# Attention with mixed heads and two feed-forward layers: heads paired j with j+6, queries in long rows, first values and small weights on GpSimd's queue, second keys at earlier steps

## The chip, the core and the metric

The kernel runs on one core of a Trainium2 chip. The core has five engines with an instruction queue each: TensorE (PE in the profile, PEld for its weight loads), VectorE (DVE), ScalarE (ACT), GpSimd (POOL) and SyncE (SP), which here only issues DMAs. The metric is the device time in microseconds (us); lower is better.

## The reference

Two batches, 12 heads, 448 positions, head size 64. The heads are mixed by a 12x12 matrix before the softmax and by another after it; two feed-forward layers follow.

```python
def _attn_ref(q, k, v, w_pre, w_post):
    scores = scale * np.matmul(q, k.transpose(0, 1, 3, 2))
    scores = np.einsum('bhij,hg->bgij', scores, w_pre)
    attn = np.exp(scores - np.max(scores, axis=-1, keepdims=True))
    attn = attn / (np.sum(attn, axis=-1, keepdims=True) + 1e-09)
    attn = np.einsum('bhij,hg->bgij', attn, w_post)
    return np.matmul(attn, v)
...
x = attn_out.transpose(0, 2, 1, 3).reshape(896, 768)
h = x @ w_in;    x = (h * np.clip(h + 3, 0, 6) / 6) @ w_out       # first layer, 768 -> 2048 -> 768
h = x @ w_in2;   x = (np.maximum(h, 0) + alpha * np.minimum(h, 0)) @ w_out2
```

## The kernel before

The attention works on eight tiles of query positions: in each batch three of 120 positions and one of 88. For a tile, `qk(ti, j)` multiplies queries and keys of two heads: head 2j in partitions 0 to 63 of the staging tiles `q_st` and `k_st`, head 2j+1 in partitions 64 to 127. Two results go through PSUM, and `s_out` copies them to the tile's scores `S`, one with ScalarE, one with VectorE (L551). Six values of j make a whole tile.

The scores are then regrouped. `pull(g)` is a DMA from `S` to a tile `pull` in which 10 positions x 12 heads lie in 120 partitions, so that the mixing over heads is a matrix product. Two groups make a step `p_`; there are 45 steps. A step runs `premix` (PE, L199, weights `wpre`), a maximum (DVE, L205), `exp` (ACT, L214), `norm` (L221 to L226, on GpSimd it scales `wpost` to `wr`), and one step later `post` (PE, L238), which mixes again and transposes, and `post_evac` (ACT, L253). In most steps from the seventh on there is also `av` (PE, L281) of a finished tile, which reads the values `v`, and in every step one `qk` of a later tile. Then come the two feed-forward layers: a weight block is loaded (`load_w`, L330), converted by ACT, DVE and GpSimd (L342 to L384) and multiplied in three passes (L451, `mm3`).

Each engine runs its instructions in the order in which the program is written. The DMAs of the main loop are all issued by SP, in order: at step `p_` the pulls for step `p_`+3, then what `load_at` has for this step (values of the first batch at steps 3, 5, 7 and 8; keys of the second batch at steps 10 to 13; values of the second batch later), then a query tile (`load_q_at`). A pull writes one of four buffers `d_buf` and waits until `premix` has read the old contents. A DMA of SP or ACT also takes one of eight semaphores in turn, so it waits until the eighth DMA before it has landed.

The opening, ahead of step 0: `load_k0` brings the first batch's keys in five DMAs and `load_q` the first two query tiles; the small weights `wpre` and `wraw` (60x60 blocks) come in between, on SP; GpSimd scales `wpre` and reorders `wraw` to `wpost` (L544, L545) when they have landed, and then clears the first four columns of the third query tile (L137), which TensorE needs for that tile. Two tiles are multiplied ahead of step 0, with their pulls behind the first of them.

In the host's layout `k0` holds head 2j+1 under head 2j, and `q` and `k` hold every head twice, in rows 0 to 63 and again in rows 64 to 127. From `q` a row of one head is 120 floats, that is 480 bytes, in one piece; from `k` 448 floats, 1792 bytes.

Of the kernel before, what the change touches and what calls it, by code (L numbers as in the profile page):

```python
# [12 lines left out]
ACTF = mybir.ActivationFunctionType  # L13
# [4 lines left out]
Q = 64  # L18
Z = 4
# [16 lines left out]
def kernel(  # L36
# [15 lines left out]
    nc = tc.nc  # L52
    _, D, H, S = k.shape
# [53 lines left out]
    with tc.manual_schedule():  # L107
# [4 lines left out]
        def load_k0(p, z, q=nc.sync):  # L112
            q.dma_start(out=k_st[0][:, p:z, :], in_=k0[:, p:z, :])

        def load_k(b, o, p, z):
            src = k[b - 1, D * o:D * o + D].rearrange("p (j o) s -> p j o s", o=2)
            nc.sync.dma_start(out=k_st[b][D * o:D * o + D, p:z, :], in_=src[:, p:z, o, :])
# [6 lines left out]
        load_k0(0, 1, nc.scalar)  # L124
        nc.vector.memset(three, 3.0)
        nc.vector.memset(warm, 0.0)
        nc.scalar.activation(out=warm, in_=warm, func=ACTF.Exp)
# [4 lines left out]
        def load_q(ti, *at, qs=(nc.sync, nc.sync)):  # L132
            T = tiles[ti]
            n = T["n"]
            m = H // 2 * n
            t = q_st[ti] = kq.tile([128, Z + H // 2 * GP], F32, tag="qst", bufs=2, name="qst")
            nc.gpsimd.memset(t[:, :Z], 0.0)  # L137
            z = Q + m - n + upper(n)
            if z > Z + m:
                nc.gpsimd.memset(t[:, Z + m:z], 0.0)  # L140
            at = (0, *at, H // 2)
            for x, y in zip(at, at[1:]):
                for o in range(2):
# [9 lines left out]
        def load_v(b, c):  # L153
            t = late.tile([128, HC, NJ, D], F32, tag=f"v{c}", bufs=1, name=f"v{c}")
            for a in range(2):
                nc.sync.dma_start(
                    out=t[Q * a:Q * a + JH], in_=v[b, JH * a:JH * a + JH, HC * c:HC * (c + 1)]
                )
            v_t[b, c] = t
# [3 lines left out]
        def qk(ti, j, tag="sc"):  # L163
            n = tiles[ti]["n"]
            if j == 0:
# [12 lines left out]
            return [(S_t[ti][:Z + n, 2 * j + o, :], ps[o][:Z + n, :S]) for o in range(2)]  # L178
# [344 lines left out]
        q0 = load_q(0, 1, 3, qs=(nc.sync, nc.scalar))  # L523
        next(q0)
        load_k0(1, 2)
        next(q0)
        load_k0(2, 3)
        load_k0(3, 4)
        next(q0)
        load_k0(4, H // 2)  # L530
        for c in range(2):
            a = GH * c
            nc.sync.dma_start(out=wpre[Z + GH * c:Z + GH * c + GH, :GH], in_=w_pre[a:a + GH, a:a + GH])
        q1 = load_q(1, 3)
        next(q1)
        for c in range(2):
            a = GH * c
            nc.sync.dma_start(out=wraw[Q * c:Q * c + GH], in_=w_post[a:a + GH, a:a + GH])
        next(q1)
# [3 lines left out]
        late.tile([128, 16], F32, tag="rest", bufs=1, name="rest")  # L543
        nc.gpsimd.tensor_scalar(wpre, wpre, scale, 1.0, ALU.mult, ALU.mult)  # L544
# [3 lines left out]

        def s_out(pairs):
# [3 lines left out]
        for j in range(H // 2):  # L553
            s_out(qk(0, j, ("sc", "mx")[j % 2]))
# [243 lines left out]
```

## Time and profile before

| | us |
|---|---|
| median of 3 runs (lowest, highest) | 665.51 (663.26, 666.89) |
| the profiled execution, its own time | 661.99 |
| its span, first to last instruction | 660.2 |
| PE busy in the span | 636.3 (96%) |
| DVE, ACT, POOL busy | 408.2, 353.2, 291.3 |
| attention, to the last `av` of the chain | about 202 |
| feed-forward layers | about 458 |

The profiled execution is one of its own; its time lies 3.52 us under the median of the other runs. The page's busy times are shares of the whole span, in which the attention and the feed-forward layers have different limits, so the stretches are read one by one. In a row of the timeline, the bracket at the end gives the engine's idle time just before and what ended it. "issue" there means that the engine waited for nothing that the profile shows.

### The profile page before, as it was taken

The numbers are of one execution on the slowest core, as the hardware profiler recorded it, in microseconds if no ns is written. First come the engines' busy times: TensorE is split into PE (matmuls) and PEld (weight loads), VectorE is DVE, ScalarE is ACT, GpSimd is POOL, SyncE is SP. The second block draws the span as 40 slices with busy tenths as digits, with TensorE's granted clock in tenths as the row PEclk, the third lists the DMA queues.
The fourth block names the chain that finished last, engine by engine and source line by source line (L and its number), as shares of the span: only waits on it lengthen the run. The fifth ranks groups of instructions, "written<-read, shape, count | busy, mean of one in ns | idle before, by whom it ended". The sixth has DMA issues, their size and how long they took to land.

```text
span 660.2 us, 17587 instructions
## 1 busy us (share of the span) xinstructions
PE 636.3 (96%) x7464; PEld 558.9 (85%) x7464; DVE 408.2 (62%) x640; ACT 353.2 (53%) x664; POOL 291.3 (44%) x236
## 2 busy tenths in 40 slices
PE   7996999998899999999999999999999999999997
PEld 2575776686688999999999999999999999999997
DVE  4664565756446678888543643389999998334501
ACT  4785787787774665666443443434444444443310
POOL 2121131312633445545675554445554556776430
PEclk9999999999899999999999999999999999999999
DMA  6776654654401233233343233212332223445202
GB/s 167 234 241 172 181 158 150 209 182 112 145 3 49 96 129 111 97 105 133 98 144 143 96 103 137 96 50 96 109 124 102 96 95 120 139 144 208 97 0 84
DMA packets 34923, 81.82 MB, mean 124 GB/s; under 512 B 11420, under 2 KB 24988, under 8 KB 34844
## 3 DMA queue, kind: packets, MB, share of 16 engines
q1 hardware_dynamic: 34268, 80.27, 37.3%
q8 instruction: 59, 0.97, 0.6%
q10 hardware_dynamic: 576, 0.41, 0.2%
q14 instruction: 20, 0.16, 0.1%
HBM read 58.65 MB, written 2.75 MB: 93 GB/s over the span
## 4 chain that ended last, share of the span: by engine, by line
PE 78%; ACT 6%; issue 5%; POOL 4%; DMA 3%; DVE 3%; SPq 0%; POOLq 0%; ACTq 0%; DVEq 0%
PE p L451 62%; PE pt L238 5%; PE mx L199 5%; PE av L281 4%; PE sc L174 3%; ACT e L214 3%; POOL wb L373 2%; POOL wlo L384 2%; ACT MT L253 1%; DMA kst<-in_k_dram 1%; DVE nm L205 1%; DVE xT L292 1%; DMA qst<-in_q_dram 1%; DMA pull<-S 1%; ACT S L551 1%
## 5 line engine op out<-in xcount | busy, mean ns | idle before, releaser
L384 POOL TENSOR_TENSOR wlo<-wb,whi 128x768 fp32r<-128x768 f32 x64 | 126.1, 1971 | 140.2 <-ACT whi L378 140.2
L373 POOL TENSOR_TENSOR wb<-wb,wst 128x768 int32<-128x768 int32 x64 | 125.6, 1963 | 74.5 <-DVE wb L366 64.9
L451 PE MATMUL p<-xh,whi 128*128 128x448 f32 x384 | 140.2, 365 | 0.0
L451 PE MATMUL p<-xl,whi 128*128 128x448 f32 x384 | 139.7, 364 | 0.0
L451 PE MATMUL p<-gl,whi 128*128 128x448 f32 x384 | 139.4, 363 | 0.0
L451 PE MATMUL p<-gh,whi 128*128 128x448 f32 x384 | 139.2, 362 | 0.0
L451 PE MATMUL p<-xh,wlo 128*128 128x448 f32 x384 | 138.5, 361 | 0.0
L451 PE MATMUL p<-gh,wlo 128*128 128x448 f32 x384 | 138.4, 360 | 0.1
L358 DVE TENSOR_SCALAR wb<-wb 128x768 f32<-128x768 f32 x64 | 52.0, 812 | 82.8 <-ACT wb L342 82.8
L342 ACT ACTIVATE wb<-wst 128x768 f32<-128x768 f32 x64 | 58.0, 907 | 70.2 <-DMA wst<-in_w_out_dram 52.2
L378 ACT CAST whi<-wb 128x768 fp32r<-128x768 f32 x64 | 53.3, 833 | 50.4 <-PE p L451 32.3
L238 PEld LDWEIGHTS pt<-wr,e 60*64 60x64 f32 (+1 forms) x2880 | 59.8, 135 | 22.1 <-issue 11.4
L214 ACT ACTIVATE e<-mx,nm 128x448 f32<-128x448 f32 x90 | 56.4, 634 | 39.8 <-DVE nm L205 39.7
L451 PEld LDWEIGHTS p<-xh,whi 128*128 128x128 f32 x384 | 72.3, 188 | 6.1
L451 PEld LDWEIGHTS p<-gh,whi 128*128 128x128 f32 x384 | 72.1, 188 | 5.7
L451 PEld LDWEIGHTS p<-gh,wlo 128*128 128x128 f32 x384 | 71.8, 187 | 5.5 <-POOL wlo L384 0.5
L451 PEld LDWEIGHTS p<-xh,wlo 128*128 128x128 f32 x384 | 72.0, 188 | 5.2
L226 POOL TENSOR_SCALAR wr<-wpost,sm 128x60 f32<-128x60 f32 x74 | 25.3, 356 | 115.4 <-DVE sm L222 112.8
L451 PEld LDWEIGHTS p<-xl,whi 128*128 128x128 f32 x384 | 72.4, 188 | 3.6
L451 PEld LDWEIGHTS p<-gl,whi 128*128 128x128 f32 x384 | 72.1, 188 | 3.7
L366 DVE SCALAR_TENSOR_TENSOR wb<-wst,wb 128x768 uint32<-128x768 uint32 x64 | 67.5, 1055 | 1.1
L238 PE MATMUL pt<-wr,e 60*64 60x60 f32 (+1 forms) x2880 | 60.7, 221 | 7.1 <-issue 6.1
(50 smaller groups left out, 792.4 us busy)
## 6 DMA issues: line engine op xcount, KB each, us to landing
wst<-in_w_out_dram SPq DMA_DIRECT2D x32, 768.0 KB
wst<-in_w_in_dram SPq DMA_DIRECT2D x27, 768.0 KB
pull<-S SPq DMA_DIRECT2D x88, 210.0 KB
wst<-in_w_in_dram SPq DMA_DIRECT2D x10, 384.0 KB
v<-in_v_dram SPq DMA_DIRECT2D x16, 168.0 KB
out_dram<-o SPq DMA_DIRECT2D x12, 224.0 KB
qst<-in_q_dram SPq DMA_DIRECT2D x8, 180.0 KB
kst<-in_k_dram SPq DMA_DIRECT2D x4, 336.0 KB
```

The costliest lines, as they stand in the source:

```text
L199: nc.tensor.matmul(ms[r][Q * c:Q * c + Q, :S], wpre[a:z], d[a:z, c, :], start=True, stop=True)
L214: nc.scalar.activation(out=e, in_=ms[o][:, :S], func=ACTF.Exp, bias=nms[o], accum_out=sm[:, o:o + 1])
L226: eng.tensor_scalar(wr, wpost, sm[:, o:o + 1], 1.0, ALU.mult, ALU.mult)
L238: nc.tensor.matmul(ts[c][Q * z:Q * z + m, u:u + GH], e[a:a + GH, j:j + m], wr[a:a + GH], start=True, stop=True,)
L281: nc.tensor.matmul(p[z][64 * o:64 * o + 64, a % 3, :n], v_t[T["b"], h // HC][Q * z:Q * z + JH, h % HC, t, :], MT[ti][Q * z:Q * z + JH, t, ...
L342: nc.scalar.activation(t, s[:, :, 1].bitcast(F32), ACTF.Abs)
L358: nc.vector.tensor_scalar(t, t, W_MAX, W_MIN, ALU.min, ALU.max)
L366: nc.vector.scalar_tensor_tensor(u, st_t[i][:, :, 1], 0xC0000000, u, ALU.bitwise_and, ALU.bitwise_or)
L373: nc.gpsimd.tensor_tensor(n, n, st_t.pop(i)[:, :, 0].bitcast(I32), ALU.add)
L378: nc.scalar.copy(hi, b_t[i])
L384: nc.gpsimd.tensor_tensor(lo, b_t.pop(i), w_t[i][0].bitcast(F32), ALU.subtract)
L451: nc.tensor.matmul(p, wt[a], xt[c], start=(first and z == 0), stop=(last and z == 2))
```

## The change

- Heads are paired j with j+6: partitions 0 to 63 hold head j, partitions 64 to 127 head j+6. The queries of one half are then contiguous in `q`: a row of a tile of 120 is one piece of 2880 bytes, and the separate rows of 480 bytes are gone. The host's layout stays as it is; each half is now read from its own copy alone. Keys of the second batch come in rows of three heads, 5376 bytes.
- The first batch's keys still lie two heads per 128 rows in `k0`, so each load becomes two DMAs of 64 partitions: slot 0, then slots 2 and 4, then slots 1, 3 and 5, and the first tile is multiplied in the order 0, 2, 4, 1, 3, 5. The first DMAs are split between SP and ACT; the table load of ACT comes after them.
- `wpre` and `wraw` are loaded by GpSimd's queue, after its memsets; the first batch's values follow there, after GpSimd's two operations on the small weights.
- The second batch's keys are loaded at steps 3, 5, 7 and 9.

On SP, the opening up to the first pulls, before (`kst` keys, `qst` queries, shapes are partitions x rows x floats):

```order
L147 DMA qst<-in_q_dram 64x120
L113 DMA kst<-in_k_dram 128x448
L147 DMA qst<-in_q_dram 64x2x120
L113 DMA kst<-in_k_dram 128x448 x2
L147 DMA qst<-in_q_dram 64x3x120
L113 DMA kst<-in_k_dram 128x896
L533 DMA wpre<-in_w_pre_dram 60x60 x2
L147 DMA qst<-in_q_dram 64x3x120 x2
L538 DMA wraw<-in_w_post_dram 60x60 x2
L147 DMA qst<-in_q_dram 64x3x120 x2
L189 DMA pull<-S 120x1x448 x2
```

and after:

```order
L115 DMA kst<-in_k_dram 64x448
L150 DMA qst<-in_q_dram 64x120
L115 DMA kst<-in_k_dram 64x2x448
L150 DMA qst<-in_q_dram 64x600
L115 DMA kst<-in_k_dram 64x3x448 x2
L150 DMA qst<-in_q_dram 64x720 x2
L191 DMA pull<-S 120x1x448 x2
```

The small weights have left SP, and the last keys of the first batch stand fifth and sixth, three heads in each.

On GpSimd, between the memsets of the `pull` buffers and the first scaling `wr` of the main loop, before:

```order
L542 MEMSET pull 4x896 x4
L544 ISA
L544 TENSOR_SCALAR wpre<-wpre 128x64
L545 COPY wpost<-wraw 128x5x12
L137 MEMSET qst 128x4
L226 TENSOR_SCALAR wr<-wpost,sm 128x60 x6
```

and after (`v_132` to `v_141` are the four value tiles of the first batch):

```order
L540 DMA wpre<-in_w_pre_dram 60x60
L541 DMA wraw<-in_w_post_dram 60x60
L540 DMA wpre<-in_w_pre_dram 60x60
L541 DMA wraw<-in_w_post_dram 60x60
L542 ISA
L542 TENSOR_SCALAR wpre<-wpre 128x64
L543 COPY wpost<-wraw 128x5x12
L158 DMA v_132<-in_v_dram 56x768 x2
L158 DMA v_135<-in_v_dram 56x768 x2
L158 DMA v_138<-in_v_dram 56x768 x2
L158 DMA v_141<-in_v_dram 56x768 x2
L141 MEMSET qst 128x4
```

Twelve DMAs stand there now, eight of them ahead of the memset of the third query tile.

On SP, from step 3 on, before:

```order
L156 DMA v_412<-in_v_dram 56x768 x2
L147 DMA qst<-in_q_dram 64x6x88 x2
L189 DMA pull<-S 120x1x448 x4
L156 DMA v_554<-in_v_dram 56x768 x2
L189 DMA pull<-S 120x1x448 x4
L156 DMA v_692<-in_v_dram 56x768 x2
L189 DMA pull<-S 120x1x448 x2
L156 DMA v_781<-in_v_dram 56x768 x2
L189 DMA pull<-S 120x1x448 x2
L147 DMA qst<-in_q_dram 64x6x120 x2
L189 DMA pull<-S 120x1x448 x2
L117 DMA kst<-in_k_dram 64x3x448
```

and after:

```order
L122 DMA kst<-in_k_dram 64x1344
L150 DMA qst<-in_q_dram 64x528 x2
L191 DMA pull<-S 120x1x448 x4
L122 DMA kst<-in_k_dram 64x1344
L191 DMA pull<-S 120x1x448 x4
L122 DMA kst<-in_k_dram 64x1344
L191 DMA pull<-S 120x1x448 x4
L122 DMA kst<-in_k_dram 64x1344
L150 DMA qst<-in_q_dram 64x720 x2
L191 DMA pull<-S 120x1x448 x10
```

The keys of the second batch stand where the values were, with four pulls between one and the next, where before they came two steps behind the last value, with two pulls between one and the next.

The diff, cut to its core:

```diff
-        def load_k0(p, z, q=nc.sync):
-            q.dma_start(out=k_st[0][:, p:z, :], in_=k0[:, p:z, :])
+        def load_k0(o, p, z, q=nc.sync):
+            for m in range(2):
+                a = p // 2 + 3 * m
+                (q[m] if isinstance(q, tuple) else q).dma_start(
+                    out=k_st[0][D * m:D * m + D, p:z:2, :],
+                    in_=k0[D * o:D * o + D, a:a + (z - p + 1) // 2, :],
+                )
-            src = k[b - 1, D * o:D * o + D].rearrange("p (j o) s -> p j o s", o=2)
-            nc.sync.dma_start(out=k_st[b][D * o:D * o + D, p:z, :], in_=src[:, p:z, o, :])
+            a = m * (H // 2)
+            nc.sync.dma_start(
+                out=k_st[b][D * m:D * m + D, p:z, :], in_=k[b - 1, D * m:D * m + D, a + p:a + z, :]
+            )
...
-                    a = T["i0"] * H
-                    src = q[T["b"], d, a:a + H * n].rearrange("p (j o n) -> p j o n", o=2, n=n)
+                    a = T["i0"] * H + o * m
                     qs[o].dma_start(
-                        out=t[d, Z + x * n:Z + y * n].rearrange("p (j n) -> p j n", n=n),
-                        in_=src[:, x:y, o, :],
+                        out=t[d, Z + x * n:Z + y * n], in_=q[T["b"], d, a + x * n:a + y * n]
                     )
...
-        q0 = load_q(0, 1, 3, qs=(nc.sync, nc.scalar))
+        q0 = load_q(0, 1, qs=(nc.sync, nc.scalar))
         next(q0)
-        load_k0(1, 2)
+        load_k0(0, 2, 5, (nc.sync, nc.scalar))
         next(q0)
...
+        load_k0(1, 1, 6)
+        list(load_q(1))
...
+            nc.gpsimd.dma_start(out=wpre[Z + GH * c:Z + GH * c + GH, :GH], in_=w_pre[a:a + GH, a:a + GH])
+            nc.gpsimd.dma_start(out=wraw[Q * c:Q * c + GH], in_=w_post[a:a + GH, a:a + GH])
...
+        for c in range(4):
+            load_v(0, c, nc.gpsimd)
...
-        for j in range(H // 2):
-            s_out(qk(0, j, ("sc", "mx")[j % 2]))
+        for i, j in enumerate((0, 2, 4, 1, 3, 5)):
+            s_out(qk(0, j, ("sc", "mx")[i % 2]))
...
-            load_at.setdefault((3, 5, 7, 8)[c], []).append(lambda c=c: load_v(0, c))
-            load_at.setdefault(10 + c, []).append(
+            load_at.setdefault(3 + 2 * c, []).append(
                 lambda c=c: load_k(1, c % 2, 3 * (c // 2), 3 * (c // 2) + 3)
             )
```

## Rows read from the trace of the kernel before

**Rows 1.** Page: instructions of each engine; DMA queue: packets, MB, share of 16 engines

```profile
PE 636.3 (96%) x7464; PEld 558.9 (85%) x7464; DVE 408.2 (62%) x640; ACT 353.2 (53%) x664; POOL 291.3 (44%) x236
...
q8 instruction: 59, 0.97, 0.6%
```

**Rows 2.** Stretches: length, busy us of PE PEld DVE ACT POOL, clock, DMA share, GB/s

```profile
10.00:15.00 5.00, 5.00 (x52) 2.06 (x49) 3.31 (x6) 2.85 (x6) 0.64 (x3) 1.00 0.33 98
...
40.00:50.00 10.00, 10.00 (x347) 8.35 (x336) 5.76 (x16) 8.04 (x22) 1.86 (x7) 1.00 0.78 235
50.00:60.00 10.00, 6.53 (x208) 4.92 (x209) 4.41 (x12) 5.46 (x14) 1.19 (x4) 1.00 0.83 184
60.00:70.00 10.00, 7.23 (x249) 5.93 (x242) 4.59 (x12) 5.93 (x16) 1.19 (x4) 1.00 0.54 171
...
210.00:410.00 200.00, 200.00 (x1002) 187.46 (x1001) 127.70 (x153) 104.82 (x151) 111.67 (x58) 1.00 0.33 111
```

**Rows 3.** Chain that ended last, 50 to 70 us: start, us, what

```profile
50.02 0.77 issue
...
54.50 2.70 issue
...
60.91 1.71 issue
...
66.52 1.06 issue
```

**Rows 4.** Timeline, 55 to 58 us: start, us, engine, line, op [idle before <-releaser]

```profile
55.82 0.60 POOL L226 TENSOR_SCALAR wr<-wpost,sm 128x60 f32<-128x60 f32 x2 [2.85 <-DVE sm L222]
...
57.20 0.49 PE L238 MATMUL pt<-wr,e 60*64 60x60 f32 x18 [2.70 <-issue]
```

**Rows 5.** DMA queues: q1 of 49.2 to 54.2 us, q8 of 54.2 to 55.2 us

```profile
q1 hardware_dynamic: 624, 1.04, 88.7%
...
q8 instruction: 1, 0.02, 8.2%
```

**Rows 6.** Timeline of SP: first and last of four loads of second keys

```profile
47.84 0.65 SPq L117 DMA_DIRECT2D kst<-in_k_dram  x1
...
61.78 0.65 SPq L117 DMA_DIRECT2D kst<-in_k_dram  x1
```

**Rows 7.** Chain that ended last, opening: last load of first keys

```profile
5.22 4.47 DMA kst<-in_k_dram
```

**Rows 8.** Timeline of ACT: first and last of eight score copies

```profile
10.83 0.53 ACT L551 COPY S<-sc 124x448 f32<-124x448 f32 x1 [0.86 <-PE sc L174]
...
16.42 0.53 ACT L551 COPY S<-sc 124x448 f32<-124x448 f32 x1 [0.22 <-PE sc L174]
```

**Rows 9.** Timeline of POOL, opening

```profile
0.97 3.18 POOL L542 MEMSET pull<- 4x896 f32 x4
...
11.20 0.29 POOL L545 COPY wpost<-wraw 128x60 f32<-128x60 f32 x1 [0.61 <-DMA wraw<-in_w_post_dram]
11.71 0.11 POOL L137 MEMSET qst<- 128x4 f32 x1 [0.22 <-PE sc L174]
```

**Rows 10.** Timeline of PE: first product of the third query tile

```profile
19.01 1.51 PE L174 MATMUL sc<-kst,qst 64*64 64x448 f32 x8 [0.63 <-DMA qst<-in_q_dram]
```

**Rows 11.** SP's issues by line: duration ns min/median/max, first and last start

```profile
L189 SPq DMA_DIRECT2D pull<-S x90: 714/780/1516, 12.3 to 168.3; - x90
...
L156 SPq DMA_DIRECT2D v<-in_v_dram x16: 363/512/1567, 26.9 to 129.8; - x16
```

**Rows 12.** Page, groups: one operation on 128x768 on POOL and on DVE

```profile
L373 POOL TENSOR_TENSOR wb<-wb,wst 128x768 int32<-128x768 int32 x64 | 125.6, 1963 | 74.5 <-DVE wb L366 64.9
...
L366 DVE SCALAR_TENSOR_TENSOR wb<-wst,wb 128x768 uint32<-128x768 uint32 x64 | 67.5, 1055 | 1.1
```

**Rows 13.** DMA queue q1: 16 to 17 us (480-byte queries), 19 to 20 (1792-byte pulls)

```profile
q1 hardware_dynamic: 498, 0.23, 94.3%
...
q1 hardware_dynamic: 149, 0.25, 65.6%
```

More of the change, by code (lines that the diff above doesn't have):

```diff
@@ L110, with load_k @@
         k_st = [kq.tile([128, H // 2, S], F32, tag=f"k{b}", name="kst") for b in range(B)]
-        def load_k0(p, z, q=nc.sync):
-            q.dma_start(out=k_st[0][:, p:z, :], in_=k0[:, p:z, :])
-        def load_k(b, o, p, z):
-            src = k[b - 1, D * o:D * o + D].rearrange("p (j o) s -> p j o s", o=2)
-            nc.sync.dma_start(out=k_st[b][D * o:D * o + D, p:z, :], in_=src[:, p:z, o, :])
+        def load_k0(o, p, z, q=nc.sync):
[5 more added lines that the diff above has]
+                )
+        def load_k(b, m, p, z):
+            a = m * (H // 2)
+            nc.sync.dma_start(
+                out=k_st[b][D * m:D * m + D, p:z, :], in_=k[b - 1, D * m:D * m + D, a + p:a + z, :]
+            )
         wraw = late.tile([128, WP], F32, tag="wraw", bufs=1, name="wraw")
@@ L123 @@
         wpost = late.tile([128, WP], F32, tag="wpost", bufs=1, name="wpost")
[L124 to L127, printed above, removed]
+        load_k0(0, 0, 1, (nc.scalar, nc.sync))
         def upper(n):
@@ L144, in load_q, with load_v @@
                     d = slice(D * o, D * o + D)
-                    a = T["i0"] * H
-                    src = q[T["b"], d, a:a + H * n].rearrange("p (j o n) -> p j o n", o=2, n=n)
+                    a = T["i0"] * H + o * m
                     qs[o].dma_start(
-                        out=t[d, Z + x * n:Z + y * n].rearrange("p (j n) -> p j n", n=n),
-                        in_=src[:, x:y, o, :],
+                        out=t[d, Z + x * n:Z + y * n], in_=q[T["b"], d, a + x * n:a + y * n]
                     )
                 yield
-        def load_v(b, c):
+        def load_v(b, c, q=nc.sync):
             t = late.tile([128, HC, NJ, D], F32, tag=f"v{c}", bufs=1, name=f"v{c}")
             for a in range(2):
-                nc.sync.dma_start(
+                q.dma_start(
                     out=t[Q * a:Q * a + JH], in_=v[b, JH * a:JH * a + JH, HC * c:HC * (c + 1)]
@@ L164, in qk @@
             n = tiles[ti]["n"]
-            if j == 0:
+            if ti not in S_t:
                 S_t[ti] = s_pool[(NTILE - 1 - ti) % 3].tile([128, H, S], F32, tag="S", name="S")
@@ L177, in qk @@
                     )
-            return [(S_t[ti][:Z + n, 2 * j + o, :], ps[o][:Z + n, :S]) for o in range(2)]
+            return [(S_t[ti][:Z + n, j + o * (H // 2), :], ps[o][:Z + n, :S]) for o in range(2)]
         d_t, mx_t, e_t, sm_t, wr_t, pt_t = {}, {}, {}, {}, {}, {}
@@ L520, in in_layer @@
             return i
-        q0 = load_q(0, 1, 3, qs=(nc.sync, nc.scalar))
+        q0 = load_q(0, 1, qs=(nc.sync, nc.scalar))
         next(q0)
-        load_k0(1, 2)
+        load_k0(0, 2, 5, (nc.sync, nc.scalar))
         next(q0)
[L527 to L539, printed above, removed]
+        nc.vector.memset(three, 3.0)
+        nc.vector.memset(warm, 0.0)
+        nc.scalar.activation(out=warm, in_=warm, func=ACTF.Exp)
+        load_k0(1, 1, 6)
+        list(load_q(1))
         for _ in range(4):
@@ L543 @@
         late.tile([128, 16], F32, tag="rest", bufs=1, name="rest")
+        for c in range(2):
+            a = GH * c
+            nc.gpsimd.dma_start(out=wpre[Z + GH * c:Z + GH * c + GH, :GH], in_=w_pre[a:a + GH, a:a + GH])
+            nc.gpsimd.dma_start(out=wraw[Q * c:Q * c + GH], in_=w_post[a:a + GH, a:a + GH])
         nc.gpsimd.tensor_scalar(wpre, wpre, scale, 1.0, ALU.mult, ALU.mult)
```

## The prediction, made before the changed kernel was run

> **What bounds the kernel now.** I read first the busy times by stretch, since the attention (to about 202 us) and the feed-forward layers have different limits. From 210 to 410 us PE is busy 200.00 of 200 us [rows 2]: the layers run at the pace of the matmuls, the change touches none of them, so whatever the attention gains or loses arrives at the end one for one. In the attention PE is full from 40 to 50 us (10.00 of 10), but has 6.53 of 10 from 50 to 60 and 7.23 of 10 from 60 to 70 [rows 2]. The chain of waits says what stands in these gaps: four pieces of "issue", 0.77, 2.70, 1.71 and 1.06 us, together 6.24 us [rows 3]. The timeline shows that they are no waits for data: the chunk of `post` that starts at 57.20 goes on in the middle of a group whose scaled weights are older, GpSimd being already at the next ones from 55.82 on [rows 4].
>
> What PE lacks there is its own instructions. The page lists 59 packets on queue q8, kind "instruction", 0.97 MB, beside 7464 + 7464 instructions of PE and PEld [rows 1]: one packet for 253 instructions. In the 5 us from 49.2 to 54.2 the queue rows hold 624 packets of data on q1, which keep the DMA engines 88.7% busy, and no q8 row; in the next microsecond q8 has one packet [rows 5], and PE runs again at 57.20. Between 40 and 50 us PE and PEld go through 347 + 336 instructions in 10 us [rows 2], so a packet lasts 253 / 68.3 = 3.7 us; a fetch that comes later than that is a gap. All four gaps lie within 5 us behind one of the four loads of second keys, 47.84 to 61.78 [rows 6]; in the steps from 3 to 8, which load values instead, the chain has none.
>
> **Term 1, the second keys.** The change moves these four loads to steps 3, 5, 7 and 9, where values were loaded, with a step between one and the next, and in rows of 5376 instead of 1792 bytes. SP's issues shrink there: eight value loads at 0.51 us leave [rows 11], four key loads at 0.65 [rows 6] come, and each is passed only by pulls that have three steps of lead; nothing waits for the keys before step 12. So the gaps at 50 to 68 us go, 6.24 us. What is late next? The same loads can hold up a fetch in their new place. Before, the gaps behind the first and the last load were 0.77 and 1.06, and the larger ones (2.70, 1.71) came where one load ran into the next. Apart, I give each the mean of the small ones, 0.92. A load of 344,000 bytes (64 x 1344 floats) takes about 1.5 us at the 235 GB/s of the stretch from 40 to 50 us [rows 2], a fetch is due every 3.7, so four in ten meet one: 4 x 0.92 x 0.4 = 1.5 us. Term 1 is -6.24 + 1.5 = **-4.7 us**. Its ends are -6.24 (no fetch is late) and 0 (all gaps come back).
>
> Weighed against a rule: the profile shows gaps of up to 2.70 us with a fetch missing. The Trainium skill (Runtime: NRT & Kernel Launch, Instruction fetch mechanics) says that crossing from one 16 KiB block of instructions to the next costs a tail-bump of the queue that is mostly hidden. By that rule the gaps would not be fetches, moving keys would bring nothing, and the sum would be term 2 alone, the time of the first rival below; [rows 3, 5] speak against it here.
>
> **Term 2, the opening.** Four parts.
>
> First keys: before, the last load (448 KB) is issued at 5.22, because it waits for an earlier one to land, and lands 4.47 us later, at 9.69 [rows 7]. Now the last two wait only for the very first two and can go some 1.5 us sooner. The bytes ahead of them are the same, so I give 0.5 us of it, between 0 and 1.5. But three pairs of heads now wait for this last landing (slots 1, 3, 5) and before two (4, 5). A pair takes (16.42 - 10.83) / 7 = 0.80 us by the score copies [rows 8]. Together +0.3, between -0.7 and +0.8.
>
> Values beside pulls: eight loads of 168 KB, 448 rows of 3072 bytes. A 1792-byte packet costs 65.6% x 16 us / 149 = 70 ns of one engine [rows 13], so a row about 121 ns and all of them 448 x 0.121 / 16 = 3.4 us of the 16 engines, which before stood at steps 3 to 8, covered by PE. From 10 to 15 us the DMA share is 0.33 [rows 2], so 3.3 us are free until the pulls need the engines, but GpSimd issues only about half of the loads by then (below). The other 1.7 us compete with the first pulls and the third query tile. Of that I take +1.0; ends 0 (hidden) and +3.4 (all ahead of the pulls).
>
> Query rows: from 16 to 17 us 498 packets of 480 bytes cost 94.3% of 16 us, 30 ns each [rows 13]; a tile of 768 is 768 x 0.030 / 16 = 1.45 us. Now it is 128 rows of 2880 bytes, by bytes 0.113 us each, 0.90 us. The 0.55 saved shortens the wait of 0.63 with which PE meets the third tile at 19.01 [rows 10]: -0.5, ends 0 and -0.6. The later five tiles I cost at nothing: they are loaded three steps ahead and PE never waits for them.
>
> GpSimd: no DMA of GpSimd is in the trace. The same value load costs SP 0.51 us of issue, and SP's longest pull issue was 1.52 [rows 11]; nothing excludes a price below 0.51 either, but it would gain nothing, since then other work ends last. I take 0.95: GpSimd needs 1963 ns where DVE needs 1055 for an operation of one size [rows 12], so 0.51 x 1.86, nearer to the row of the same DMA. The memsets end at 0.97 + 3.18 = 4.15, the four small loads are issued by 8.0, `wpost` is ready at the latest when it is now, 11.5 [rows 9], and the eight value loads end between 16.1 and 19.1. Behind them in GpSimd's order stands the memset of the third query tile, at 11.71 before [rows 9], and PE's product waits for it: due at 19.01 before [rows 10], at 19.8 now with the rest of this term. So it is just covered, at 0; with `wpost` at 11.5 the cover ends at (19.8 - 11.6) / 8 = 1.03 us an issue, and at 1.52 it costs 4.0 us. SP's load of that tile doesn't wait for the new memset.
>
> Term 2 is 0.3 + 1.0 - 0.5 = **+0.8 us**, between -1.3 and +4.2, and +8 with the dearest issues.
>
> **Sum.** -4.7 + 0.8 = -3.9: the profiled execution of 661.99 us becomes 658.1. The median of the runs, 665.51, lies 3.5 higher; the same shift gives **661.6 us**.
>
> **Rivals.**
>
> *The gaps move with the keys.* For it: the new steps carry as many pulls, and at steps 3 and 9 a query tile is loaded right behind the keys. Against it: the loads stand apart, and values of the same size at these steps left no gap. Then term 1 is 0 and the time 665.51 + 0.8 = 666.3.
>
> *The opening gains too and no fetch is late.* For it: SP's queue is shorter by seven issues up to the first pulls, and half of the DMA time is free from 10 to 15 us. Term 1 is -6.24, term 2 -1.3: 658.0.
>
> *GpSimd holds up PE.* The place is the memset of the third query tile behind the eight value loads; from 1.03 us an issue it costs eight times the excess, and from about 1.52 us it has eaten all of the gain. For it: DVE is busy 3.31 of 5 us from 10 to 15 [rows 2], copying scores. Were GpSimd to issue only while DVE rests (34% of the time), an issue would take 0.95 / 0.34 = 2.8 us, the loads would end at 11.5 + 22.4 = 33.9 and the memset come 14 us late: 661.6 + 14 = 675.6, slower than before. Against it: `wpost` took 0.29 at 11.20 while DVE copied [rows 9]. The Trainium skill (SBUF — State Buffer, SBUF: two separate sides) states that a DMA issued from GpSimd is starved of descriptors while DVE runs an operation in a two-port mode, and names the fp32 copy from SBUF to SBUF; the copies here read PSUM, so by that rule it would not come to this, and no row here has a GpSimd DMA to try it on.
>
> **How the numbers follow.** Forecast 0.50, gaps move 0.20, opening gains too 0.18, GpSimd holds up PE 0.12. A measurement of this kernel can tell a change of about 0.5%, 3.3 us. The forecast has its middle 3.9 under the old median and an uncertainty of some 2 us, so 0.30 of its 0.50 is faster, 0.19 no change, 0.01 slower; the second case is no change (0.18) or slower (0.02); the third faster (0.17, the rest no change); of the last 0.02 is no change and 0.10 slower. That makes faster 0.47, same 0.40, slower 0.13. The range goes from 657.0 (the third case and a microsecond of spread) to 668.5 (the second with a dear opening); the long end of the last case and the tails of the others are left out.
>
> **What would show each step.** Term 1: in the profile of after, the PE busy time of the ten microseconds that hold steps 10 to 13 rises to 9.7 or more, and "issue" in the chain behind the key loads at steps 3 to 9 sums to about 1 us. If it sums to 5, the second case is right. Term 2: SP issues the first pull between 0.1 earlier and 0.6 later than now; GpSimd's value loads take 0.7 to 1.1 us each and end before 19.5; `premix` of step 1 comes less than 1.5 us later than now. The prediction is wrong if PE waits for GpSimd at the third query tile, if the pulls of step 1 are over 2 us late, or if the attention's later steps, which I left as they are, fall into another rhythm.

## The result, and the profile after

The changed kernel is slower by 0.6%: median 667.9 us of 17 runs (665.24 to 672.49), beside 664.62 of 17 runs of the kernel before; the ratio is 1.0063, 95% interval 1.0039 to 1.0086. The profiled execution took 666.48 us (span 664.6), 4.49 more than the one before. The forecast was 661.6, faster; its range, 657.0 to 668.5, holds the time, its direction is wrong.

To see where the time goes I compare the start of `premix` at each step, that is every eighth of the 360 products of its line (L199, now L201).

| `premix` of step | before | after | difference |
|---|---|---|---|
| 0 | 17.05 | 22.37 | +5.32 |
| 1 | 20.43 | 27.98 | +7.55 |
| 6 | 34.60 | 42.87 | +8.27 |
| 10 | 47.88 | 57.72 | +9.84 |
| 14 | 68.06 | 72.72 | +4.66 |
| 44 | 186.99 | 191.38 | +4.39 |

So the opening loses 7.55 us, steps 1 to 10 another 2.29; steps 10 to 14, where the gaps of [rows 3] were, give back 5.18; the rest gives back another 0.27. The sum, +4.39, is the difference of the spans (4.4).

The chain of waits of the changed kernel (start, us, what) has in the opening two waits for transfers that answer to [rows 7, 10], and these gaps behind it:

```profile
2.96 4.88 DMA qst<-in_q_dram
7.98 6.79 PE sc L176 x46
...
15.93 8.79 DMA pull<-S
...
41.78 0.46 issue
...
46.33 1.71 issue
...
60.01 0.35 issue
...
71.75 0.49 issue
```

PE's second pair now waits for the queries of five pairs in one DMA; then both first steps wait for their pulls. The timeline of the same stretch:

```profile
12.72 0.30 POOL L543 COPY wpost<-wraw 128x60 f32<-128x60 f32 x1 [0.39 <-DMA wraw<-in_w_post_dram]
13.21 4.18 POOL L158 DMA_DIRECT2D v<-in_v_dram  x8 [0.19 <-issue]
14.89 1.84 SPq L191 DMA_DIRECT2D pull<-S  x2
16.91 1.17 SPq L150 DMA_DIRECT2D qst<-in_q_dram  x2
17.38 0.13 POOL L141 MEMSET qst<- 128x4 f32 x1
...
22.37 1.72 PE L201 MATMUL mx<-pull,wpre 64*64 64x448 f32 x2 [3.14 <-DMA pull<-S]
24.75 1.12 PE L201 MATMUL mx<-pull,wpre 64*64 64x448 f32 x3 [0.67 <-DMA pull<-S]
```

SP's first pull is 2.56 us later than in [rows 11], GpSimd issues the value loads from 13.21 to 17.39, at the same time, and the first `premix` has its pull only at 22.37. The stretches (columns as in [rows 2]):

```profile
10.00:15.00 5.00, 5.00 (x44) 2.14 (x40) 3.12 (x6) 2.64 (x6) 2.33 (x6) 1.00 0.36 85
15.00:20.00 5.00, 4.22 (x40) 1.55 (x34) 3.69 (x6) 2.98 (x6) 2.50 (x6) 1.00 0.86 235
20.00:25.00 5.00, 1.97 (x5) 0.53 (x8) 0.00 (x0) 0.00 (x0) 0.00 (x0) 0.71 0.77 193
25.00:30.00 5.00, 5.00 (x30) 1.98 (x33) 2.54 (x6) 1.76 (x5) 0.60 (x2) 0.60 0.66 241
...
40.00:50.00 10.00, 7.83 (x207) 5.26 (x204) 5.23 (x13) 6.79 (x18) 1.81 (x6) 1.00 0.73 220
50.00:60.00 10.00, 10.00 (x348) 8.85 (x339) 5.76 (x16) 8.09 (x22) 1.84 (x7) 1.00 0.66 201
60.00:70.00 10.00, 9.57 (x306) 7.79 (x309) 5.78 (x15) 8.21 (x22) 1.80 (x6) 1.00 0.39 144
```

PE idles 3 of the 5 us from 20 on, its granted clock falls, and when the pulls come it works at 0.60 for a while: 5.00 us at 0.60 is the work of 3.0, so up to 2 us of the loss is this. From 50 to 70 us PE is nearly full, about as forecast.

### The profile page after: what moved, and what is told of

Read it like the earlier page. It is cut to its first block, busy times and chain, and to the rows that moved or that the text cites. A ratio compares the mean times of both kernels' runs of the same rounds, so it can differ in the third digit from the quotient of the medians.

```text
span 664.6 us, 17594 instructions
## 1 busy us (share of the span) xinstructions
PE 638.0 (96%) x7464; PEld 560.5 (84%) x7464; DVE 408.1 (61%) x640; ACT 353.9 (53%) x664; POOL 298.4 (45%) x248
## 3 DMA queue, kind: packets, MB, share of 16 engines
HBM read 58.65 MB, written 2.75 MB: 92 GB/s over the span
## 4 chain that ended last, share of the span: by engine, by line
PE 77%; ACT 7%; issue 5%; POOL 4%; DVE 3%; DMA 2%; SPq 0%; ACTq 0%; POOLq 0%; DVEq 0%
PE p L453 61%; PE mx L201 4%; PE av L283 4%; PE pt L240 4%; ACT e L216 4%; PE sc L176 3%; POOL wb L375 2%; POOL wlo L386 2%; ACT MT L255 2%; DMA pull<-S 1%; DVE nm L207 1%; DMA qst<-in_q_dram 1%; DVE xT L294 1%; ACT S L552 1%; ACT xT L293 0%
## 5 line engine op out<-in xcount | busy, mean ns | idle before, releaser
L207 DVE TENSOR_REDUCE nm<-mx 128x1 f32<-128x448 f32 x90 | 52.1, 618 | 29.3 <-PE mx L201 29.3
```

Of the source, the lines that this page charges most:

```text
L207: nc.vector.tensor_reduce(nm, m[:, :S], axis=AX.X, op=ALU.max, negate=True)
```

## The experiments

Each run was compared with the kernel before in the same session; the last three columns are read from its trace.

| run | ratio (95%) | step 1 starts | steps 6 to 10 | steps 10 to 14 |
|---|---|---|---|---|
| before, two traces | 1 | 20.43, 19.73 | 13.28, 13.98 | 20.18, 20.29 |
| after, two traces | 1.0063 (1.0039, 1.0086) | 27.98, 27.65 | 14.85, 13.85 | 15.00, 15.62 |
| e1 values and keys back | 1.0036 (1.0005, 1.0066) | 23.37 | 13.28 | 20.45 |
| e2 values later | 1.0138 (1.0101, 1.0175) | 22.39 | 25.97 | 14.82 |
| e3 before, values early | 1.0038 (1.0008, 1.0067) | 25.96 | 13.03 | 15.43 |
| e4 before, no second keys | 0.9974 (0.9948, 0.9999) | 20.17 | 13.38 | 15.57 |
| e5 before, new pairs | 1.0042 (1.0014, 1.0069) | 21.04 | 13.48 | 19.89 |
| e7 before, keys in twelve | 0.9980 (0.9949, 1.0012) | 20.37 | 13.26 | 19.14 |
| e8 before, values by GpSimd | 1.0047 (1.0018, 1.0077) | 19.47 | 17.90 | 14.19 |
| e9 = e1, warm products | 0.9986 (0.9958, 1.0015) | 22.54 | 13.29 | 18.93 |
| e10 before, warm products | 1.0007 (0.9973, 1.0042) | 20.50 | 14.32 | 21.24 |
| e11 before, half values early | 1.0039 (1.0002, 1.0075) | 23.23 | 13.69 | 17.54 |
| e12 before, stride nine | 0.9991 (0.9965, 1.0017) | 20.26 | 14.18 | 22.18 |
| e13 before, keys early | 1.0046 (1.0023, 1.0069) | 20.35 | 13.52 | 22.73 |
| e14 = e7 + e12; again, e16 | 0.9962 (0.9937, 0.9986); 0.9963 (0.9933, 0.9992) | 19.27, 21.00 | 14.51, 13.23 | 15.47, 17.81 |
| e15 = e9 + e7 + e12 | 0.9999 (0.9967, 1.0031) | 21.33 | 13.12 | 18.10 |
| e17 before, no first values | 0.9957 (0.9929, 0.9986) | 20.28 | 12.81 | 16.95 |

### How much of a trace comes again

Both kernels, unchanged, a second time (the times were 665.65 and 667.40 us).

> The kernel before, unchanged, profiled a second time, to see how much of a trace comes again. If the gaps have their places from the program and its transfers: the steps start within 0.5 us of the first trace up to step 10, and steps 11 to 13 show 5 to 7 us of issue again. If they fall by chance: the sum from step 10 to 14 differs by over 2 us, and the single trace says little of what a change moves.

> The changed kernel, unchanged, profiled a second time. If its losses and gains have their places from the program: premix of step 1 again 7 to 8 us later than in the kernel before, a gap of 1.5 to 2.5 us at steps 7 to 9, 3 to 6 us won back from step 10 to 14. If they fall by chance: the opening's 7 us come again, but the gap at steps 7 to 9 is under 1 us or the gain from 10 to 14 under 2.

The second trace of the kernel before differs by up to 0.9 us to step 11, and single steps behind it take up to 2.2 us more or less; from step 10 to 14 it takes 20.29 us again, with 0.97 and 3.31 us of issue in its chain there, less than the 5 to 7 expected. By step 44 it is 3.65 us behind the first trace, so the last row of the table above depends on which traces are compared. The changed kernel loses 7.92 us at step 1 again and gains from step 10 to 14 again (15.62); its gap at steps 7 to 9 was 0.9 us instead of 2.2. So single gaps, of 1 or 2 us, can't be compared. Sums over four steps can, but only roughly: e12 below differs from the kernel before only in the tiles of 88, from step 15 on, and takes 22.18 us from step 10 to 14, and the two traces of one kernel, e14 and e16, take 15.47 and 17.81. A difference of 2 us in the last column may be chance.

### The values beside the first pulls

The changed kernel without the moves of values and keys:

```diff
-        for c in range(4):
-            load_v(0, c, nc.gpsimd)
...
-            load_at.setdefault(3 + 2 * c, []).append(
+            load_at.setdefault((3, 5, 7, 8)[c], []).append(lambda c=c: load_v(0, c))
+            load_at.setdefault(10 + c, []).append(
```

> The changed kernel with the first values back on SP at steps 3, 5, 7 and 8 and the second keys back at steps 10 to 13; its opening stays. Theory (the values on GpSimd's queue crowd out the first pulls, the changed order of the opening costs some 2.5 us by itself): the first pull is still issued near 14.9 us, but premix of step 1 starts near 23 instead of 27.98; the gaps of the kernel before (about 6 us of issue in the chain) come back with the keys; 666.5 us in all, 1 to 2.5 over the kernel before. Rival (the late first tile alone carries the whole loss, and the transfers of the values only fill time that is lost anyway): premix of step 1 stays at 27 to 28 and the time is 671.

Step 1 at 23.37: 4.61 of the 7.55 us are gone with the values, 2.95 stay with the opening. (e2 below has the same opening up to step 1 and starts it at 22.39; by that trace it is 5.59 and 1.96.) The converse, the kernel before with its first values on GpSimd's queue ahead of the loop (and its SP loads of them taken out), and the same with two of the four tiles:

```diff
+        for c in range(4):
+            load_v(0, c, nc.gpsimd)
+
         def s_out(pairs):
...
-            load_at.setdefault((3, 5, 7, 8)[c], []).append(lambda c=c: load_v(0, c))
```

> The kernel before with one change, the first values on GpSimd's queue ahead of the main loop; nothing goes to steps 3 to 8 instead. Theory: the first pull stays at 12.3 us, but premix of step 1 comes at 24 to 26 instead of 20.43, the gaps behind the second keys at steps 10 to 13 stay; 668 to 669 us. Rival (values beside the pulls are hidden): premix of step 1 at 20.5 to 21.5 and 664.6, no change.

> The kernel before with the first two of the four value tiles on GpSimd's queue ahead of the main loop, the other two on SP at steps 7 and 8. Theory (from 13 to 26 us the transfers run at their limit of some 250 GB/s, so early values cost their bytes: all four, 1.38 MB, cost 5.53 us at step 1): 0.69 MB cost 2.75 us, premix of step 1 at 22.7 to 23.6; 664 to 665.5. Rival A (a fixed price of the second queue): 5 us, as with all four. Rival B (half of it fits into the free time from 10 to 15 us): under 1 us.

All four cost 5.53 us at step 1, two cost 2.81. The time of e3 was 666.03 us, not 668 to 669, and the gaps of steps 10 to 13 did not stay as forecast (15.43 us). Queues and timeline of e3 (in the queue rows packets, MB, and their time as a share of 16 engines, from 13 to 26 us), then the queue row of e11 and the first products of `premix` in it and in the kernel before:

```profile
q0 software_dynamic: 384, 1.38, 43.2%
q1 hardware_dynamic: 1390, 1.36, 39.7%
...
12.69 1.80 SPq L189 DMA_DIRECT2D pull<-S  x2
...
22.73 1.76 PE L199 MATMUL mx<-pull,wpre 64*64 64x448 f32 x6 [2.49 <-DMA pull<-S]
```

```profile
q0 software_dynamic: 192, 0.69, 19.9%
...
19.10 2.67 PE L199 MATMUL mx<-pull,wpre 64*64 64x448 f32 x8 [2.20 <-DMA pull<-S]
```

```profile
17.05 1.33 PE L199 MATMUL mx<-pull,wpre 64*64 64x448 f32 x8 [0.37 <-issue]
```

43.2% of 13 us are 5.6 us of all engines, 19.9% are 2.6: each is close to the delay at step 1. By packet it is 5.6 x 16 / 384 = 0.234 us for 3.6 KB, 65 ns per KB, where the pulls cost 39 [rows 13]. The delay is not all waiting, though. While PE waits, its granted clock falls (0.50 from 20 to 25 us in e3, the lower of its levels, 0.73 in e11, 1.00 in the kernel before). In e11 the wait for the pull puts step 0 off by 2.05 us; the other 0.76 come while its eight products take 2.67 us instead of 1.33. The Trainium skill (DMA: Bandwidth & Descriptors, Queues, rings and completion order) says that a DMA engine takes turns between queues, packet by packet. The traces agree in that both queues run at once (q0 61.1% and q1 33.9% of the engines from 18 to 20 us in the changed kernel); that turns make the delay is not shown. Bytes at the 250 GB/s that the pulls reach here give nearly the same delay, and the runs don't tell the two apart.

Later on the same queue, in the loop:

```diff
-        for c in range(4):
-            load_v(0, c, nc.gpsimd)
...
+            if p_ in (1, 2, 4, 6):
+                load_v(0, (1, 2, 4, 6).index(p_), nc.gpsimd)
             if 1 <= p_:
                 post(p_ - 1)
```

> The changed kernel with the first values still on GpSimd's queue, but issued in the main loop at steps 1, 2, 4 and 6. Theory (the place in time, not the queue, costs): premix of step 1 near 23 us, the rest of the later order of the opening (2.5) is left and the shorter gaps (-2.5 to -3.5) are kept: 664 us, between the two kernels' times or a little below the one before. Rival (the late first tile carries it): 668, as the changed kernel. A second rival (values at these steps meet the keys at steps 3 to 9 and hold up the fetch of PE's instructions again): premix of step 1 near 23, but 4 us or more of issue in the chain from 30 to 60 us, 666.

The opening is as in e1 (step 1 at 22.39), but the run is the slowest. The chain has one wait of 9.74 us for a pull, and the stretch is nearly full of transfers:

```profile
32.92 9.74 DMA pull<-S
42.66 2.19 issue
```

```profile
30.00:40.00 10.00, 8.19 (x240) 5.65 (x236) 6.69 (x16) 8.86 (x24) 3.86 (x12) 1.00 0.94 208
```

Values and keys together, 2.75 MB within nine steps, are more than the pulls leave room for. The gaps behind it (2.19, 1.12 and 4.50 us up to 60 us) are those of the second rival; the wait for the pull none of the three had. Is it the queue? The kernel before with its values at their own steps, issued by GpSimd:

```diff
-append(lambda c=c: load_v(0, c))
+append(lambda c=c: load_v(0, c, nc.gpsimd))
```

> The kernel before with the first values at the same steps 3, 5, 7 and 8, but issued by GpSimd instead of SP. Theory (what costs in the changed kernel is the time at which the values move, not the queue): premix of steps 5 to 10 within 1 us of the kernel before and 663 to 665. Rival (GpSimd's queue lets the values pass the pulls, which on SP's queue they share in order): premix of step 9 or 10 3 us or more later, 667 or more; then the second run with values at steps 1, 2, 4 and 6 was slow for its queue.

```profile
46.00 2.80 issue
```

Partly: the chain has this gap, and step 10 is 3.79 us late, as the rival says; from step 6 to 14 it is 32.09 us, no more than the 33.46 before. The trace ends where the first one before ends, yet the runs are 0.47% slower: the profiled execution, 661.97 us, was the shortest of the twelve. What the others lose stays open.

### The opening without the values

Eight products of zeros ahead of the first queries, in e1 (e9) and in the kernel before (e10):

```diff
+        nc.vector.memset(k_st[1][:, 0, :], 0.0)
+        pw = psA.tile([128, 512], F32, tag="pt", bufs=2, name="pw")
+        for i in range(8):
+            r = D * (i % 2)
+            nc.tensor.matmul(
+                pw[r:r + Q, :S], k_st[1][r:r + D, 0, :Q], k_st[1][r:r + D, 0, :], start=True, stop=True
+            )
```

> The run with the values back (the changed kernel's opening, values and second keys as before), with eight products of zeros on PE ahead of the first queries, from about 1 us on; their result is not used. Theory (the later opening is a matter of PE's clock: its products last 951 ns up to about 14 us there and 536 after it, in the kernel before only up to about 7.7 us, because PE began later and waited longer): the products of the first tile last under 600 ns from 8 us at the latest, the first pull is issued near 13 instead of 15.81, premix of step 1 starts at 20.5 to 21.5 instead of 23.38, 663.5 to 664.5 in all. Rival (the order in which keys and queries land sets it): premix of step 1 stays within 0.5 us of 23.4, 666.

> The kernel before with the same eight products of zeros. Theory (clock): products of 536 to 560 ns from about 4 us on instead of 7.7; the last keys still land at 9.7, so premix of step 1 gains 0.3 to 1.0 us on 20.43; 662.5 to 663.5. Rival (the opening is bound by the landings alone): within 0.2 us, 664.

The products of `qk` (count: shortest/median/longest ns, start of the first and last) from 7 to 9 us in the kernel before, from 11.5 to 13.5 in e1, from 7 to 9 in e9:

```profile
L174 PE MATMUL sc<-kst,qst x20: 536/570/951, 6.6 to 9.0; 64*64 64x448 f32 x10, 64*60 64x448 f32 x10
```

```profile
L176 PE MATMUL sc<-kst,qst x16: 824/951/951, 10.6 to 13.4; 64*64 64x448 f32 x8, 64*60 64x448 f32 x8
```

```profile
L176 PE MATMUL sc<-kst,qst x16: 536/536/583, 6.5 to 8.9; 64*64 64x448 f32 x8, 64*60 64x448 f32 x8
```

The same product lasts 951 ns or 536, as the Trainium skill (TensorE: Matmul & The Clock Gate, What's actually happening) has it of the two levels, 1.2 and 2.4 GHz: low after rest, high after work. (The column of the granted clock reads 1.00 even there, as in e1's stretch below.) In e1 PE began 1.6 us later, waited 0.94 us for queries at 8.12 and stayed at the low level to about 14 us.

```profile
5.00:10.00 5.00, 3.77 (x20) 1.70 (x24) 0.62 (x1) 0.63 (x2) 1.40 (x3) 1.00 1.07 244
```

With e9's products the first pull goes at 14.36 instead of 15.81, and step 0 gains 1.66 us of the 3.43, step 1 0.83 of the 2.95. That is between the theory (step 1 at 20.5 to 21.5) and its rival: about half of the loss at step 0 is the clock, and less than a third at step 1. What is left stands beside landings, which remain: in e9 PE still waits for queries at 7.97 and for keys at 10.95. In the kernel before, where the last keys land at 9.7 anyway, the products gain nothing; there they also stand in the way, since the first product of queries starts at 5.98 instead of 3.70.

Pairs and long rows alone, in the old order of the opening:

```diff
-        "k0": k[0].reshape(H // 2, 2, S, D).transpose(1, 3, 0, 2).reshape(2 * D, H // 2, S),
+        "k0": k[0].reshape(2, H // 2, S, D).transpose(0, 3, 1, 2).reshape(2 * D, H // 2, S),
```

with `load_q`, `load_k` and the index of `S` as in the change.

> The kernel before with the pairs j, j+6 and the 2880-byte query rows alone: keys of the first batch in the host's layout by these pairs, so that the opening keeps its five key loads of 128 rows, its three pieces of the first query tile and its order; small weights and values on SP, second keys at steps 10 to 13. Theory (the order of the first loads costs the 2.95 us at step 1 that the run with the values back showed, the pairing none): the first pull is issued by 12.3 us, the third query tile waits less, premix of step 1 starts at 19.7 to 20.2; gaps behind the second keys as before; 663 to 664, no change or 0.1% less. Rival (the pairs or the long rows themselves cost it): premix of step 1 near 23, 666 to 667.

Nearer to the theory than to its rival (21.04), but no gain: the wait for the third query tile was 0.77 us, not less than the 0.63 of [rows 10], since its transfer runs among the pulls. PE's products were at the low level to 11.6 us and the first pull was issued at 13.70, where twelve traces with the old pairs and opening have 7.4 to 10.4 and 11.9 to 13.2. So the new pairs or rows probably have a part in it; it is one trace, and nothing separates the two.

### What makes the gaps of steps 10 to 14

Four ways to take the traffic away. Second keys left out (`k_ = k_st[0]` for both batches, and no `load_k`):

> The kernel before without the four loads of second keys: the second batch is multiplied with the first batch's keys, so this computes something else; all other instructions stay. Theory (the gaps of 6.24 us from 50 to 68 us are PE's instructions that come late behind these loads): issue in the chain between 48 and 70 us falls below 1 us, PE is busy over 9.5 of 10 us from 50 to 60 and from 60 to 70, and the time is 658.5, 6 us less. Rival (the gaps belong to the place in the program, or move on to the next load): issue of 4 us or more stays there or comes in the 20 us behind, 663 to 664.6.

The second keys moved, and nothing else:

```diff
-            load_at.setdefault(10 + c, []).append(
+            load_at.setdefault(3 + 2 * c, []).append(
```

> The kernel before with the second keys at steps 3, 5, 7 and 9 and nothing else: the first values stay on SP at steps 3, 5, 7 and 8, ahead of them. The time from premix of step 6 to that of step 14 was 33.46 us in the first trace of the kernel before, 34.27 in the second, 29.85 in the changed kernel. If the keys' place is the cause, as the prediction had it: 29 to 30 us, and 660.5 in all. If the sum of the transfers in steps 3 to 13 is (values and keys, 2.75 MB beside the pulls): 32 to 34 us, with gaps that come earlier, from step 7 on, and 663.5 to 665.5.

The second keys in small pieces:

```diff
+        for c in range(H):
+            load_at.setdefault(4 + c, []).append(
+                lambda c=c: load_k(1, c % 2, c // 2, c // 2 + 1)
+            )
```

> The kernel before with the second keys in twelve loads of one slot and half (64 rows of 1792 bytes, 115 KB), one at each step from 4 to 15, instead of four of 344 KB at steps 10 to 13. Theory (a fetch of PE's instructions waits behind what one large load has queued): the 16.2 us between the premix of steps 10 and 13 shrink to 12 to 13 and nothing new of that size comes: 661. Rival (what counts is the traffic in sum, and a gap avoided at one place comes at the next heavy one): 663.5 to 665, with new issue gaps at steps 5 to 9 or behind step 14.

The first values left out, the keys where they were:

```diff
+            if b == 0:
+                nc.gpsimd.memset(t, 0.0)
-            for a in range(2):
+            for a in range(2 * b):
                 nc.sync.dma_start(
```

> The kernel before without the eight loads of first values at steps 3 to 8; GpSimd clears these tiles instead, so the first batch's output is another. The second keys stay at steps 10 to 13. If the gaps come from a backlog of transfers (values, keys and pulls together keep the DMA engines at their limit from 20 to 60 us): DMA share from 40 to 50 us falls from 0.78 to 0.5, the time from premix of step 10 to that of step 14 falls from 20.2 to 16 to 17.5 us, and 660 to 662 in all. If a key load beside a fetch makes them: 19.5 to 20.5 us remain there, 663.5 to 664.5.

Without the keys the four steps take 15.57 us, without the values 16.95 (as e17's theory had it), with the keys moved away 22.73: no less than before, and e13's runs are 0.46% slower. That is worse than either forecast of e13; e12's 22.18 without any change there says that the trace alone does not show an increase. Here is e13's chain and its stretches; its last key load is issued at 49.28.

```profile
51.20 2.40 issue
...
57.31 4.44 issue
```

```profile
30.00:40.00 10.00, 9.45 (x253) 6.53 (x250) 6.26 (x16) 9.09 (x23) 2.41 (x8) 1.00 0.91 215
40.00:50.00 10.00, 10.00 (x341) 8.59 (x336) 6.05 (x15) 8.11 (x22) 1.88 (x7) 1.00 0.81 213
50.00:60.00 10.00, 4.91 (x165) 3.36 (x157) 4.47 (x11) 4.82 (x13) 1.20 (x4) 0.99 0.85 191
60.00:70.00 10.00, 8.25 (x179) 6.34 (x183) 2.66 (x7) 4.08 (x10) 0.60 (x2) 0.66 0.34 129
```

The gap of 4.44 us stands 8 us behind the last key load, while the engines are still 85% busy. It is a late fetch too: no packet of instructions is in the queue rows from 55 to 59.2 us, one is from 59 to 60, and PE goes on at 61.75. And e17, whose key loads stand at 48.27 to 58.69 as before (stretches, then its chain):

```profile
30.00:40.00 10.00, 9.81 (x263) 6.91 (x266) 6.55 (x16) 8.78 (x23) 2.94 (x9) 1.00 0.54 181
40.00:50.00 10.00, 10.00 (x343) 8.99 (x340) 5.74 (x15) 8.46 (x23) 3.31 (x10) 1.00 0.58 178
50.00:60.00 10.00, 9.59 (x331) 7.90 (x325) 6.49 (x16) 7.83 (x22) 1.53 (x6) 1.00 0.76 225
...
62.71 2.06 issue
```

PE is nearly full from 50 to 60 us beside the same keys, and one gap is left. So the first values have a part in the gaps, though they land before them. How, is argued and not shown. It may be a backlog: values, keys and pulls together keep the transfers at 235 to 242 GB/s from 20 to 50 us in the kernel before (181 and 178 here from 30 to 50), and the fetches would come late at the end of that. It shows in steps 10 to 13 and not earlier, I think, because PE then goes through its code faster (347 + 336 instructions from 40 to 50 us [rows 2]); no run varied that. The stretches ahead of it in the kernel before:

```profile
20.00:30.00 10.00, 10.00 (x250) 6.33 (x248) 7.00 (x18) 7.54 (x22) 1.88 (x8) 1.00 0.67 242
30.00:40.00 10.00, 10.00 (x290) 7.40 (x288) 7.46 (x18) 9.17 (x25) 2.40 (x8) 1.00 0.75 242
```

Against a mere backlog stands the second trace of the changed kernel, which moves nearly as much for longer, and has two gaps over 0.2 us before 60 us, of 0.48 and 1.04:

```profile
30.00:40.00 10.00, 10.00 (x308) 7.12 (x306) 7.50 (x19) 9.51 (x27) 2.06 (x9) 1.00 0.75 236
40.00:50.00 10.00, 9.52 (x280) 7.08 (x275) 6.12 (x16) 8.49 (x23) 2.06 (x8) 1.00 0.76 229
50.00:60.00 10.00, 8.96 (x331) 7.50 (x327) 6.27 (x16) 7.73 (x21) 1.46 (x7) 1.00 0.71 222
```

Cutting the loads small didn't change it clearly (19.14).

A gap that is avoided may come again. In e4 steps 10 to 14 save 4.61 us, but then its chain has this, steps 14 to 22 take 34.58 us instead of 30.55, and the runs are only 0.26% faster, not the 6 us forecast:

```profile
84.37 2.90 issue
```

Around it the pulls of the tile of 88 positions are slow. The last experiment on that changes the stride of these pulls from 8 partitions to 9:

```diff
-            st = n // G
+            st = -(-n // G)
             for g in range(st):
-                groups.append((t, g, st, G))
-            if n % G:
-                groups.append((t, st * G, 1, n % G))
+                groups.append((t, g, st, len(range(g, n, st))))
```

with `post_evac`, `av` and `by_row` following the new groups.

> The kernel before with one change elsewhere: the tile of 88 positions is cut into nine groups with a stride of 9 partitions (seven of 10 positions, two of 9) instead of eight with a stride of 8 and one of 8 neighbours. Its pulls (for steps 18 to 22 and 40 to 44) had packets of 133 ns, in two of the runs of 253 ns, where those of other tiles take 74. Theory (stride 8 is what makes them slow, and a fetch of PE's instructions behind them is late): 74 ns, no issue gap between steps 14 and 21, 1 to 3 us less: 661 to 663. Rival (the pulls have three steps of lead and the gaps are not theirs): packets of 74 ns, but 663.5 to 664.5; or the packets stay at 133 and the stride is not the cause.

The queue rows from 84 to 86 us, the kernel before, then e12:

```profile
q1 hardware_dynamic: 117, 0.19, 41.6%
```

```profile
q1 hardware_dynamic: 119, 0.21, 27.5%
```

41.6% x 16 x 2 us / 117 is 114 ns a packet, 27.5% gives 74: the stride is what made them slow. The time did not move (0.9991): the first traces of the kernel before and of e12 take the same from step 14 to 22 (30.55 and 30.74 us), so these pulls were covered by their lead of three steps.

### A version below both

e7 and e12 together, and with the opening of e9:

> The kernel before with the second keys in twelve loads at steps 4 to 15 and with stride 9 in the tiles of 88 positions; each alone measured 0.2% and 0.1% below the kernel before, neither surely. If the two add up: 662 to 663, a ratio of 0.997. If each was chance: 664 to 665, 1.000.

> The run with the warm products (pairs j and j+6, long query rows, the changed opening behind eight products of zeros, values on SP) with the twelve key loads and stride 9 as well. If the parts add up: 0.995 to 0.997 of the kernel before, 661.5 to 663, and about 1% below the changed kernel. If they don't: 0.998 to 1.000, 663.5 to 665.

> The version with twelve key loads and stride 9 a second time, since it was the lowest of several. If its 0.38% is its own: a ratio of 0.994 to 0.999 again. If it was the luck of the draw: 0.999 to 1.002.

e14 is 0.38% below the kernel before, and 0.37% when measured again; 0.9962 / 1.0063 puts it about 1.0% below the changed one. Its steps 10 to 14 took 15.47 and 17.81 us, in an execution of 658.88 us, the shortest of its twelve, and in one of 664.81. Which of its two edits shortens them, when neither does so clearly alone, is not settled. e15 came out even.

## Why the prediction was wrong

**The step that failed is term 2, the opening: +0.8 by the sum, 7.55 in the trace.** Two of its four parts were mis-sized.

*Values beside pulls* (+1.0, ends 0 and 3.4): measured 4.61 (after against e1) and 5.53 (e3). Two errors. The price was taken by rows of pulls and keys, 3.4 us of the engines, and is 5.6. And I counted the DMA share short of 1 as free time and let only 1.7 us compete. But the values were issued from 13.21 on and the pulls from 14.89, so the two met almost entirely. The half dose (2.81 for 5.53) shows no free part of any size. What neither the sum nor its ends had is the clock that PE loses while it waits, 0.76 of the 2.81 in e11.

*First keys* (+0.3, ends -0.7 and +0.8): the whole opening without the values cost 2.95 (e1; 1.96 by e2's trace). I had looked at the last key's landing. What came late was the first tile's queries: five pairs in one DMA, which landed at 7.84, so that PE's second pair ran at 7.98 instead of 5.8. And I took the 0.80 us of a pair from [rows 8], a stretch at the high clock; the late start kept PE at the low one, at 951 ns a product.

*Query rows* (-0.5): nothing was gained (e5). *GpSimd* (0 at 0.95 us an issue): right in the result; an issue took 4.18 / 8 = 0.52 us, and the memset came at 17.38, long ahead of PE. The third rival is refuted by that. The rule weighed there (the Trainium skill, SBUF — State Buffer, SBUF: two separate sides) was not put to its own case: DVE was busy 3.12 and 3.69 us of 5, but with copies out of PSUM, and no issue of a value load shows a delay.

**Term 1, -4.7, came out in size and not in cause.** From step 6 to 14 the changed kernel takes 29.85 us for 33.46, in the second traces 29.47 for 34.27: -3.6 and -4.8. That the gaps are late fetches stands. But I tied them to the key load next to each, and e13 shows that moving the keys alone does not take them away. The sizes (small behind a load that stands apart) were no rule either: in the second trace the 3.31 us stand 5.8 us behind the last load. What removed them in the changed kernel is, by e3 and e17, that its values are out of the way by step 3: e3 leaves the keys in place and takes 15.43 us from step 10 to 14, so the move of the keys added nothing to that. "In the steps with value loads the chain has none" was read the wrong way round: these loads have a part in the gaps that come later. A part of the gain may be only the opening's loss given back. That it is all of it is unlikely: e17, not late and without values, takes 16.95 us, and e1, 2.95 us late with values and keys in place, takes 20.45. The first rival, that the gaps move along with the keys, is wrong for the same reason; that its 666.3 lies nearest to the measured 667.9 is luck.

Of the signs that were named: PE in ten microseconds of steps 10 to 13, forecast at 9.7 or more, 9.57 from 60 to 70, just short; "issue" at steps 3 to 9, about 1 us, 0.46 + 1.71, higher; SP's first pull, at most 0.6 later, 2.56, wrong; GpSimd's value loads, 0.7 to 1.1 us each and done before 19.5, 0.52 and 17.39, cheaper and in time; `premix` of step 1, under 1.5 later, 7.55, wrong, and with pulls over 2 us late this was the case named as the one that makes the prediction wrong.

## What to carry to other kernels

Price an early transfer by the engine time of its own kind of packet, and add all of it where a chain of transfers is being waited for: a DMA share below 1 is not free time for it. An event that shortly follows a load needs a run with that load alone moved before the load is called its cause; here loads of 20 us earlier had a part in it. In an opening, a product that waits can also keep PE longer at its low level, and a wait in mid-program can send it back there. Where single traces of one kernel differ by 2 us over four steps, a trace is read beside the runs' times.

## What the runs showed of the hardware

- The granted clock in the profile reads 1.00 in the first 14 us, while the same product lasts 951 ns and later 536; only the duration shows the low level. In twelve traces with the same opening the last product at that level ended between 7.4 and 10.4 us.
- Pulls from every eighth partition take 114 ns a packet between 84 and 86 us, from every ninth 74.
- In e13 a late fetch of instructions stops PE for 4.44 us, in a stretch in which the DMA engines are 85% busy with data.
- GpSimd issues a value load in 0.52 us, no more than SP [rows 11], but its packets of 3.6 KB cost the DMA engines 65 ns per KB beside the pulls, and 59 from 13.2 to 14.8 us in e3, where no other queue starts a packet; a pull's cost 39.
